# One scratch buffer for the first rotation, and the third token block's row sums ahead of the last pair's tokens

## The chip, the core and the metric

The kernel runs on one core of a Trainium2 chip. The metric is the device time of one execution in microseconds (us). Before the change its median is 719.28 us over 3 runs (718.72 to 720.0).

A core has five engines, each with its own queue of instructions that it takes in order: TensorE (PE in the profile; matmuls and transposes), VectorE (DVE), ScalarE (ACT), GpSimd (POOL) and SyncE (SP, which here only issues transfers). TensorE's weight loads are listed apart as PEld. Transfers are carried out by DMA engines, which all queues share. An instruction can wait on counters ("semaphores") that other engines or landed transfers raise.

## The reference

Attention with rotary embedding over 4 batches, 8 heads, 576 positions and head size 64, and then a gated feed-forward layer over the 2304 tokens that attention gives (512 wide, 1536 hidden), all in float32:

```
q_rot, k_rot = (rotate(q), rotate(k))          # x1*cos - x2*sin, x1*sin + x2*cos
scores = q_rot @ k_rot^T / sqrt(64);  scores -= max;  attn = exp(scores)
attn = attn / (sum(attn) + 1e-9);     x = attn @ v  -> [2304, 512]
g = x @ w_gate;   silu = g / (1 + exp(-g));   val = x @ w_val
out = (silu * val) @ w_out
```

## The kernel before

Values are split into a high and a low part (`hi`, `lo`), and each product is made of two or three matmuls on the parts. The 32 heads are worked on as 16 pairs of heads. A pair has 9 blocks of 128 query rows; each block is scored against all 576 keys, its row maximum is taken (VectorE, L358), the exponential is taken with row sums (ScalarE, L376), E is transposed (TensorE, L419), split again (L420, L421), and multiplied with the values (L459). The unnormalised results go to a DRAM area `yd`, the reciprocals of the row sums to a DRAM area `rd`. The feed-forward part then loads tokens from `yd`, multiplies them with row sums from `rd`, splits them and runs the gate and value products (12 "units" by plain products, L776; the rest with a scheme of seven block products, L824), and at last the output product (L892, L941).

The opening, `start` (L210), rotates the first pair. The rotation `turn` (L182) makes four tensor-tensor steps: two products with the sine table into a scratch (L200), one with the cosine table into `rot` (L201), one add (L202). Keys and the first quarter of the queries are rotated by VectorE (L229, L232), the other three quarters of the queries by GpSimd (L233). VectorE's scratch `tp` and a small scaled table `td` are taken from the pool of scores buffers (`sc_p`, two buffers of 128x1024 in PSUM), which are not yet in use. ScalarE fills `td` (L230) and the scaled query table `tab[0]` (L231), which GpSimd's rotation reads. TensorE then transposes keys, tails and the first query quarter, ScalarE and VectorE split them (L302, L306), and `scores(0)` runs; then the three other query quarters are transposed (L253), and `scores(1)`, `scores(2)` follow. The order on each engine in `start` is as written, up to small moves by the scheduler.

The second place is `plain` (L1196), the first part of the feed-forward layer. At its start (L1227 to L1234) SyncE issues loads in the order written: weights, tokens of blocks 1 and 2 of the second batch pair for the first three head pairs of each batch (`yload(1, 0)`, `yload(2, 0)`), row sums (`rload(1, 1)`, and `rload(1, 2)` into `R12`, a piece of buffer `T2l`), and the tokens of the last head pair of each batch (`yload(1, 1)`, `yload(2, 1)`). `rload` (L602) for the third token block issues six loads, `yload` (L632) four: two into `T0h` (`Ya`), two into `T2h` (`Yb`). `xlate(1)` and `xlate(2)` (L640) then combine them: for each of four groups c, ScalarE copies Ya (L649), VectorE adds Yb (L650) and multiplies with the row sums (L651), ScalarE and VectorE split (L656, L659). `ev(u)` (L780) empties a unit's PSUM on ScalarE (L791, L792) and issues its store from ScalarE's own queue (L799, L802).

Transfers are counted with eight counters, named DMAHW0 to DMAHW7 in the order below. They are given out in turn to transfers of SyncE and ScalarE alike, and the instruction that issues a transfer waits until the transfer before it on the same counter has landed. The suffixes on names, as in `yd_58`, are buffer numbers.

Of the kernel before, what the change touches and what calls it, by code (L numbers as in the profile page):

```python
# [10 lines left out]
FP32 = mybir.dt.float32  # L11
# [6 lines left out]
B, H, S, D = 4, 8, 576, 64  # L18
# [77 lines left out]
def r32(ap):  # L96
    return ap.bitcast(FP32)
# [10 lines left out]
class Attn:  # L108
# [101 lines left out]
    def start(self):  # L210
        nc = self.nc
        ve, po = nc.vector, nc.gpsimd
        rot = self.rot[0] = self.rot_p.tile([128, NSLOT, D], FP32, name="rot")
        rf = rot.rearrange("p s d -> p (s d)")
        T = nc.tensor.transpose
        tr = lambda: self.tr_p.tile([128, 512], FP32, name="tr")
        hi = lambda *x: self.qk_hi(0, *x)
        lo = lambda *x: self.qk_lo(0, *x)
        pw = self.pv_p.tile([128, 512], FP32, name="pv")

        def warm(n):
            for _ in range(n):
                nc.tensor.matmul(pw[:, 0:128], self.ident, self.ident, start=True, stop=True)
        w = PLAN["warm"]
        nc.scalar.copy(self.et_p.tile([128, 640], FP32, name="Et")[:, 0:1], r32(self.BD[0])[:, 0, 0:1])
        warm(w[0])
        self.turn(po, 0, 2)
        tp, td = (self.sc_p.tile([128, 1024], FP32, name="sc").rearrange("p (s d) -> p s d", d=D) for _ in range(2))
        self.turn(ve, 0, 1, 0, 4, tp[:, 0:8])  # L229
        nc.scalar.mul(td[:, 0:2], self.tab[1][:, :, 0], float(D ** -0.5))  # L230
        nc.scalar.mul(self.tab[0], self.tab[1], float(D ** -0.5))  # L231
        self.turn(ve, 0, 0, 0, 1, tp[:, 8:10], td[:, 0:2, None])  # L232
        self.turn(po, 0, 0, 1, 4)  # L233
        pk, pt, pq = tr(), tr(), tr()
        kt = lambda i: T(pk[:, i * 128:(i + 1) * 128], rf[:, 512 + i * 128:640 + i * 128], self.ident)
        for o in (64, 0):
            T(pt[:, o:o + 128], rf[:, 1024:1152], self.ident)
        warm(w[1])
        for i in range(4):
            kt(i)  # L240
        warm(w[2])
        T(pq[:, 0:128], rf[:, 0:128], self.ident)
        for x in ((pt, None, 192), (pk, 640, 512), (pq, 64, 128)):
            hi(*x)
        for x in ((pt, None, 192), (pk, 640, 512), (pq, 64, 128)):
            lo(*x)
        nc.scalar.copy(self.VS[0][:, :, 0:64], self.VR)
        warm(w[3])
        self.scores(0, False, lambda x: warm(w[4]) if x == 0 else None)
        self.peak(0)  # L250
        ps = tr()
        for i in range(1, 4):
            T(ps[:, i * 128:(i + 1) * 128], rf[:, i * 128:(i + 1) * 128], self.ident)  # L253
        self.scores(1, False)
        hi(ps[:, 128:512], 192, 384)
        lo(ps[:, 128:512], 192, 384)
        self.peak(1)
        self.exp(0)
        self.exp(1)
        warm(w[5])  # L260
        self.scores(2)
        self.exp(2)
        del self.rot[0], self.X[0]
        self.load_qk(2)
        self.qk_stack(0)
# [708 lines left out]
def attn_swiglu(ctx: ExitStack, tc: tile.TileContext, qk, vr, wg, wv, wo, main, tail, out):  # L974
# [163 lines left out]
    moe.open_chain(cctx, 2, side="right")  # L1138
    moe.open_aux(xctx, 2)
    J, S, Z = plain(moe, ps, cv1[1])  # L1140
    mctx.close()
    pl.close()
# [12 lines left out]
def run(ops, n=99):  # L1155
    while ops and n:
        ops.pop(0)()
        n -= 1
# [37 lines left out]
def plain(moe, ps, first):  # L1196
    nc = moe.nc
    ve, po = nc.vector, nc.gpsimd
    J = [Conv(moe, 1 + s // 2, s % 2, s % 2) for s in range(10)]
    jobs = []  # L1200

    def job(kind, x, h=0):
        if kind == "w":
            jobs.append((lambda: J[x].load(h), lambda: J[x].bits(h, ve)))
        else:
            jobs.append((lambda: moe.oload(x), lambda: moe.obits(x)))

    for s in range(10):
        for h in range(2):
            job("w", s, h)  # L1210
        if s in (4, 6, 8):
            job("o", 2 + s // 2)
    for f in (0, 1, 2, 3, 7, 8, 9, 10, 11):
        job("o", f)
    S = Stream(moe, jobs)
    ps = {1: ps}

    def mm(u):
        ps[u] = [moe.mm(*UNITS[u], i) for i in range(2)]

    def ev(u):
        moe.ev(u, ps.pop(u))

    def T1(c):
        run(moe.split(ve, *(t[:, :, c] for t in moe.T[1]), moe.Z[c]))

    S.load()  # L1227
    S.load()
    moe.yload(1, 0)
    moe.rload(1, 1)  # L1230
    moe.yload(2, 0)
    moe.yload(1, 1)
    moe.rload(1, 2, moe.R12)
    moe.yload(2, 1)  # L1234
    run(first())
    for c in range(2):
        run(moe.forms(1, c, moe.Z[c], po))
    x1, x2 = moe.xlate(1), moe.xlate(2)
    mm(2)
    S.sign()  # L1240
    run(S.take(1))
    ev(1)
    mm(3)
    run(S.take(1, False))
    run(J[0].sums(po))
    ev(2)
    mm(4)
    ev(3)
    mm(5)
    run(x1, 5)  # L1250
    ev(4)
    mm(6)
    run(x1)
    ev(5)
    mm(7)
    T1(0)
    run(x2, 3)
    ev(6)
    mm(8)
    w = [J[0].split(x, po) for x in range(2)]  # L1260
    run(w[0])
    run(x2, 2)
    ev(7)
    mm(9)
    run(w[1])
    run(x2)
    ev(8)
    mm(10)
    T1(1)
    Z = [moe.r_p.tile([128, 4, BK], FP32, name="R"), moe.again("T0l0", [128, 4, BK], FP32, "Z")]  # L1270
    for c in range(2):
        run(moe.forms(0, c, Z[c], po))
    T2 = moe.forms2(ve)
    run(T2, 2)
    ev(9)
    mm(11)
    run(T2)
    ev(10)
    S.sign()
    run(S.take(1))  # L1280
    ev(11)
    return J, S, Z
# [106 lines left out]
```

## Time and profile before

| what | value |
|---|---|
| median of 3 runs | 719.28 us |
| profiled execution, its own time | 719.76 us |
| its span, first to last instruction | 717.9 us |
| PE busy | 697.0 us (97%), 4342 matmuls |
| DVE / ACT / POOL busy | 540.6 / 409.6 / 476.8 us |
| mean granted TensorE clock | 0.994 of full speed |
| DMA | 143.86 MB, mean 200 GB/s |

The span leaves out 1.86 us that the device time holds (719.76-717.9). A timeline row gives the start and the duration in us, the engine, the line of the kernel, the operation, what it writes and reads, and in brackets how long the engine had been idle before it and what ended that. "SPq" and "ACTq" are the queues that issue transfers. A busy TensorE is not TensorE at its peak, and matmuls overlap, so the duration of a group includes its drain.

### The profile page before, as it was taken

The numbers are of one execution on the slowest core, as the hardware profiler recorded it, in microseconds if no ns is written. First come the engines' busy times: TensorE is split into PE (matmuls) and PEld (weight loads), VectorE is DVE, ScalarE is ACT, GpSimd is POOL, SyncE is SP. The second block draws the span as 40 slices with busy tenths as digits, with TensorE's granted clock in tenths as the row PEclk, the third lists the DMA queues.
The fourth block names the chain that finished last, engine by engine and source line by source line (L and its number), as shares of the span: only waits on it lengthen the run. The fifth ranks groups of instructions, "written<-read, shape, count | busy, mean of one in ns | idle before, by whom it ended". The sixth has DMA issues, their size and how long they took to land.

```text
span 717.9 us, 12738 instructions
## 1 busy us (share of the span) xinstructions
PE 697.0 (97%) x4342; PEld 656.7 (91%) x4342; DVE 540.6 (75%) x884; ACT 409.6 (57%) x892; POOL 476.8 (66%) x473
## 2 busy tenths in 40 slices
PE   7999999999999999998899999999999999999997
PEld 6999999999999998988899999999999877888887
DVE  5889898898898887848988778778677893464451
ACT  5889988888888886357433534424243332432331
POOL 8899799999999966649966576655675767200000
PEclk9999999999999999999999999999999999999999
DMA  6798899779887896862355555645638865787671
GB/s 195 195 232 204 218 227 253 199 202 249 233 215 196 201 269 165 248 202 101 121 168 171 177 163 173 193 147 165 185 115 272 280 245 169 306 284 223 205 220 30
DMA packets 111330, 143.86 MB, mean 200 GB/s; under 512 B 17809, under 2 KB 86049, under 8 KB 111265
## 3 DMA queue, kind: packets, MB, share of 16 engines
q1 hardware_dynamic: 106576, 137.64, 67.5%
q10 hardware_dynamic: 4688, 5.39, 2.3%
q8 instruction: 35, 0.57, 0.3%
q14 instruction: 31, 0.25, 0.1%
HBM read 76.35 MB, written 42.54 MB: 166 GB/s over the span
## 4 chain that ended last, share of the span: by engine, by line
PE 64%; DMA 10%; POOL 10%; DVE 8%; ACT 5%; issue 2%; SPq 1%; ACTq 0%; DVEq 0%; POOLq 0%
PE ch L824 28%; PE ch L941 13%; PE sc L343 7%; PE pv L459 6%; PE tr L419 5%; DMA HF<-hf 3%; PE ch L892 2%; POOL t L200 1%; DMA raw<-in_moe_w_gate_dram 1%; DMA QK<-N 1%; POOL rot L202 1%; DMA ht<-sv 1%; POOL rot L201 1%; PE tr L283 1%; POOL Xab L628 1%
## 5 line engine op out<-in xcount | busy, mean ns | idle before, releaser
L358 DVE TENSOR_REDUCE nmt<-sc 128x1 f32<-128x576 f32 x144 | 108.1, 751 | 20.0 <-PE sc L343 18.4
L376 ACT ACTIVATE E<-sc,nmt 128x576 f32<-128x576 f32 x128 | 97.3, 760 | 1.6 <-DVE nmt L358 1.4
L808 POOL TENSOR_TENSOR u<-u,z 128x384 f32<-128x384 f32 x30 | 30.5, 1018 | 72.9 <-DVE sg L808 72.9
L419 PE MATMUL tr<-ident,E 128*128 128x128 f32 x512 | 77.1, 273 | 0.5 <-DVE ET1l L421 0.2
L419 PEld LDWEIGHTS tr<-ident,E 128*128 128x128 f32 x512 | 61.1, 141 | 3.4 <-PE tr L283 1.3
L827 ACT COPY c<-ch 128x384 f32<-128x384 f32 x30 | 14.4, 480 | 84.7 <-PE ch L824 50.2
L200 POOL TENSOR_TENSOR t<-X,tab 128x256 f32<-128x256 f32 (+2 forms) x94 | 54.2, 597 | 10.1 <-DMA X<-in_qk_dram 6.4
L343 PE MATMUL sc<-QK 128*128 128x288 f32 x240 | 58.6, 325 | 1.7 <-ACT E L376 0.4
L420 ACT CAST ET2h<-tr 128x512 fp32r<-128x512 f32 x80 | 47.1, 589 | 15.5 <-PE tr L419 15.4
L421 DVE TENSOR_TENSOR ET2l<-tr,ET2h 128x512 fp32r<-128x512 f32 x80 | 53.1, 682 | 2.2 <-ACT ET2h L420 2.0
L678 DVE TENSOR_TENSOR hl<-hg,hh 128x384 fp32r<-128x384 f32 x44 | 25.8, 587 | 37.6 <-ACT hh L678 37.6
L941 PE MATMUL ch<-Oh,hh 128*128 128x512 f32 (+1 forms) x144 | 54.0, 375 | 0.0
L941 PE MATMUL ch<-Oh,hl 128*128 128x512 f32 (+1 forms) x144 | 53.9, 374 | 0.0
L941 PE MATMUL ch<-Ol,hh 128*128 128x512 f32 (+1 forms) x144 | 53.8, 374 | 0.0
L343 PE MATMUL sc<-N,QZ 128*128 128x288 f32 x240 | 51.3, 295 | 0.0
L202 POOL TENSOR_TENSOR rot<-rot,t 128x512 f32<-128x512 f32 (+2 forms) x47 | 47.0, 1000 | 3.7
L421 DVE TENSOR_TENSOR ET1l<-tr,ET1h 128x512 fp32r<-128x512 f32 x64 | 43.0, 685 | 6.8 <-ACT ET1h L420 6.5
L201 POOL TENSOR_TENSOR rot<-X,tab 128x512 f32<-128x512 f32 (+2 forms) x47 | 47.0, 1001 | 0.0
L808 DVE TENSOR_TENSOR sg<-ch,u 128x384 f32<-128x384 f32 x60 | 33.4, 556 | 16.5 <-PE ch L824 13.3
L678 ACT CAST hh<-hg 128x384 fp32r<-128x384 f32 x44 | 22.6, 514 | 39.3 <-DVE hg L928 39.3
L420 ACT CAST ET1h<-tr 128x512 fp32r<-128x512 f32 x64 | 36.9, 597 | 13.0 <-PE tr L419 13.0
L459 PE MATMUL pv<-ET2h,VS 128*128 128x320 f32 x128 | 40.7, 328 | 1.0 <-ACT ET2h L420 0.9
(413 smaller groups left out, 2418.9 us busy)
## 6 DMA issues: line engine op xcount, KB each, us to landing
QK<-N SPq DMA_DIRECT2D x64, 288.0 KB, 4.4
hg<-ht SPq DMA_DIRECT2D x22, 768.0 KB, 6.8
HF<-hf SPq DMA_DIRECT2D x12, 896.0 KB, 5.1
X<-in_qk_dram SPq DMA_DIRECT2D x15, 576.0 KB, 4.9
yd<-Y SPq DMA_DIRECT2D x31, 256.0 KB, 4.4
ht<-sg SPq DMA_DIRECT2D x20, 384.0 KB, 3.7
hf<-sg SPq DMA_DIRECT2D x20, 384.0 KB, 3.8
ht<-sg SPq DMA_DIRECT2D x20, 320.0 KB, 3.1
```

The costliest lines, as they stand in the source:

```text
L200: e.tensor_tensor(out=sel(t2, u), in0=sel(x, w), in1=tb(Sn, u), op=ALU.mult)
L201: e.tensor_tensor(out=o, in0=x, in1=tb(C, slice(0, D)), op=ALU.mult)
L343: nc.tensor.matmul(ps[:, g, 0:288], l, rr[:, o + g * 288:o + (g + 1) * 288], start=(x == 0), stop=(x == len(terms) - 1))
L358: nc.vector.tensor_reduce(out=nmcol, in_=ps[:, :, 0:288], axis=AX.XY, op=ALU.max, negate=True)
L376: nc.scalar.activation(out=E.rearrange("p (a b) -> p a b", a=2), in_=ps[:, :, 0:288], func=ACTF.Exp, bias=nmcol, scale=1.0, accum_out=self ...
L419: nc.tensor.transpose(ps[:, c], E[:, o + c * 128:o + (c + 1) * 128], self.ident)
L420: nc.scalar.copy(dst[0], src)
L421: nc.vector.tensor_tensor(out=dst[1], in0=src, in1=r32(dst[0]), op=ALU.subtract)
L459: nc.tensor.matmul(st["ps"][:, 0:w], VS[:, sl, :], t, start=(x == 0), stop=(x == last))
L808: add = lambda e, out, in0, in1: e.tensor_tensor(out=out, in0=in0, in1=in1, op=ALU.add)
L824: nc.tensor.matmul(acc, l[:, w, c * 128:(c + 1) * 128], r, start=(n == 0), stop=(n == 5))
L941: self.nc.tensor.matmul(ps, l[:, f], r[:, z], start=(n == 0), stop=(n == 3 * NFF - 1))
```

## The change

Two edits. In `start`, `td` is no longer a buffer of its own but columns 640 to 767 of the buffer that holds `tp`. In `plain`, the six loads of `rload(1, 2)` are issued ahead of the four of `yload(1, 1)`.

```
-        tp, td = (self.sc_p.tile([128, 1024], FP32, name="sc").rearrange("p (s d) -> p s d", d=D) for _ in range(2))
+        tp = self.sc_p.tile([128, 1024], FP32, name="sc").rearrange("p (s d) -> p s d", d=D)
+        td = tp[:, 10:12]
         self.turn(ve, 0, 1, 0, 4, tp[:, 0:8])
         nc.scalar.mul(td[:, 0:2], self.tab[1][:, :, 0], float(D ** -0.5))
         nc.scalar.mul(self.tab[0], self.tab[1], float(D ** -0.5))
         self.turn(ve, 0, 0, 0, 1, tp[:, 8:10], td[:, 0:2, None])
@@
     moe.yload(2, 0)
+    moe.rload(1, 2, moe.R12)
     moe.yload(1, 1)
-    moe.rload(1, 2, moe.R12)
     moe.yload(2, 1)
```

Line numbers after the first edit are one higher than before. On ScalarE, in the opening, the rows were these (a row: line, operation, output and inputs, shape, what it waits for); `sc<-tab_98` fills `td`, `tab_97` is the scaled query table:

```order
L225 COPY Et<-BD_95 128x1 [waits DVE_49]
L230 ACTIVATE sc<-tab_98 128x128 [waits DMAHW2_49]
L231 ACTIVATE tab_97<-tab_98 128x512
L302 CAST N_93<-tr 128x3x64 [waits PE_49]
L302 CAST N_93<-tr 128x512 [waits PE_49]
```

On ScalarE at the same place they are now:

```order
L225 COPY Et<-BD_95 128x1 [waits DVE_49]
L231 ACTIVATE sc<-tab_98 128x128 [waits DMAHW2_49,DVE_49]
L232 ACTIVATE tab_97<-tab_98 128x512
L303 CAST N_93<-tr 128x3x64 [waits PE_49]
L303 CAST N_93<-tr 128x512 [waits PE_49]
```

Nothing moved; the step that fills `td` has a wait for VectorE (`DVE_49`) that it did not have. On VectorE, in the opening, the rotation's rows were these:

```order
L201 TENSOR_TENSOR rot<-X,tab_98 128x2x4x64
L202 TENSOR_TENSOR rot<-rot,sc 128x2x4x64 [waits DVE_49]
L200 TENSOR_TENSOR sc<-X,sc 128x2x32 [waits DMAHW4_49,DVE_49,Activation_49]
L200 TENSOR_TENSOR sc<-X,sc 128x2x32 [waits DVE_49]
L201 TENSOR_TENSOR rot<-X,sc 128x128
L202 TENSOR_TENSOR rot<-rot,sc 128x128 [waits DVE_49]
```

On VectorE at the same place they are now:

```order
L201 TENSOR_TENSOR rot<-X,tab_98 128x2x4x64
L202 TENSOR_TENSOR rot<-rot,sc 128x2x4x64 [waits DVE_49]
L200 TENSOR_TENSOR sc<-X,sc 128x2x32 [waits DMAHW4_49,Activation_49]
L200 TENSOR_TENSOR sc<-X,sc 128x2x32 [waits DVE_49]
L201 TENSOR_TENSOR rot<-X,sc 128x128 [waits DVE_49]
L202 TENSOR_TENSOR rot<-rot,sc 128x128 [waits DVE_49]
```

The first `sc<-X,sc` waits for ScalarE alone of the two engines, and the step that reads `td` next has a wait for VectorE's own earlier step. On TensorE the third scores, `scores(2)`, and the first transposes of E that follow stood in this order; they are now interleaved, with two of the four transposes ahead of the last two score matmuls (two lines of the order, four transposes before as `x4`, now twice `x2`). On ScalarE the exponential of the sixth block now stands ahead of a cast of pair 1's rotated rows (L302) that stood before it. On GpSimd no row moved.

On SyncE, in `plain`, the rows from the last load of `yload(2, 0)` on were these (the ten that change places are the second to the eleventh; `T2l<-rd` is `rload(1, 2)`, `T0h` and `T2h` from `yd_58` first `yload(1, 1)`, then `yload(2, 1)`):

```order
L638 DMA T2h<-yd_57 64x3x384 [waits DMAHW4_49]
L638 DMA T0h<-yd_58 64x384 [waits DMAHW5_49]
L638 DMA T2h<-yd_58 64x384 [waits DMAHW6_49]
L638 DMA T0h<-yd_58 64x384 [waits DMAHW7_49]
L638 DMA T2h<-yd_58 64x384 [waits DMAHW0_49]
L613 DMA T2l<-rd 64x4x256 [waits DMAHW1_49,DVE_49,PE_49]
L613 DMA T2l<-rd 64x4x256 [waits DMAHW2_49]
L613 DMA T2l<-rd 64x4x64 [waits DMAHW3_49]
L613 DMA T2l<-rd 64x4x64 [waits DMAHW4_49]
L613 DMA T2l<-rd 64x4x64 [waits DMAHW5_49]
L613 DMA T2l<-rd 64x4x64 [waits DMAHW6_49]
L638 DMA T0h<-yd_58 64x384 [waits DMAHW0_49]
```

On SyncE at the same place they are now:

```order
L639 DMA T2h<-yd_57 64x3x384 [waits DMAHW4_49]
L614 DMA T2l<-rd 64x4x256 [waits DMAHW5_49,DVE_49,PE_49]
L614 DMA T2l<-rd 64x4x256 [waits DMAHW6_49]
L614 DMA T2l<-rd 64x4x64 [waits DMAHW7_49]
L614 DMA T2l<-rd 64x4x64 [waits DMAHW0_49]
L614 DMA T2l<-rd 64x4x64 [waits DMAHW1_49]
L614 DMA T2l<-rd 64x4x64 [waits DMAHW2_49]
L639 DMA T0h<-yd_58 64x384 [waits DMAHW3_49]
L639 DMA T2h<-yd_58 64x384 [waits DMAHW4_49]
L639 DMA T0h<-yd_58 64x384 [waits DMAHW5_49]
L639 DMA T2h<-yd_58 64x384 [waits DMAHW6_49]
L639 DMA T0h<-yd_58 64x384 [waits DMAHW0_49]
```

The six row-sum loads moved ahead of four token loads. The counters stay with the places: place two uses number 6 and place ten uses it again, whichever transfer stands there.

On ScalarE the store of `ev(5)`, `hf<-Xab` (L799), takes counter 6 next after the tenth load of these lists, before and now. Some rows ahead of it, ScalarE's copy of the last token group (L649, c=3) waits for counter 5 before, and now for counters 5 and 3: the loads at places nine and seven. VectorE's add behind it (L650) waits for the two `T2h` loads of the same `yload(1, 1)`, now at places eight and ten.

## Rows read from the trace of the kernel before

**Rows 1.** Busy time by stretch: span, then busy us of each engine, clock, DMA.

```profile
20.00:260.00 240.00, 236.38 (x1856) 228.72 (x1854) 211.63 (x342) 212.99 (x539) 221.17 (x255) 1.00 0.86 218
```

**Rows 2.** Timeline of the opening, all engines: start, duration, engine, line.

```profile
5.31 0.28 ACT L230 ACTIVATE sc<-tab 128x128 f32<-128x128 f32 x1 [2.17 <-DMA tab<-in_rope_dram]
...
5.53 0.61 ACT L231 ACTIVATE tab<-tab 128x512 f32<-128x512 f32 x1
...
6.28 1.53 POOL L200 TENSOR_TENSOR t<-X,tab 128x192 f32<-128x192 f32 x2 [1.32 <-ACT tab L231]
...
6.84 0.69 DVE L202 TENSOR_TENSOR rot<-rot,sc 128x512 f32<-128x512 f32 x1
...
7.58 0.65 PE L235 MATMUL tr<-ident,rot 128*128 128x128 f32 x4 [0.45 <-DVE rot L202]
7.62 0.49 DVE L200 TENSOR_TENSOR sc<-X,sc 128x64 f32<-128x64 f32 x2
...
8.84 1.00 POOL L202 TENSOR_TENSOR rot<-rot,t 128x384 f32<-128x384 f32 x1
...
9.38 1.05 PE L343 MATMUL sc<-N 64*128 64x288 f32 x6
...
10.37 0.55 PE L253 MATMUL tr<-ident,rot 128*128 128x128 f32 x3
...
13.23 0.42 PEld L419 LDWEIGHTS tr<-ident,E 128*128 128x128 f32 x4 [0.17 <-issue]
```

**Rows 3.** Timeline of SyncE's queue: the ten loads that change places.

```profile
299.09 0.47 SPq L638 DMA_DIRECT2D T0h<-yd  x1
303.96 0.47 SPq L638 DMA_DIRECT2D T2h<-yd  x1
...
305.53 0.44 SPq L638 DMA_DIRECT2D T2h<-yd  x1
306.08 4.33 SPq L613 DMA_DIRECT2D T2l<-rd  x6
```

**Rows 4.** Timeline of VectorE (first row) and ScalarE around the store.

```profile
308.02 0.57 DVE L650 TENSOR_TENSOR aux<-aux,T2h 128x384 f32<-128x384 f32 x1 [0.89 <-ACT aux L649]
...
307.50 0.48 ACT L649 COPY aux<-T0h 128x384 f32<-128x384 f32 x1 [0.48 <-DVE xa2l L659]
...
310.34 0.50 ACT L792 COPY Xab<-ch 128x384 f32<-128x384 f32 x1
314.94 0.34 ACTq L799 DMA_DIRECT2D hf<-Xab  x1
315.33 1.47 ACT L678 CAST T1h<-T0l 128x1536 fp32r<-128x1536 f32 x1 [4.49 <-DMA T2l<-rd]
...
320.45 0.51 ACT L791 ACTIVATE Xab<-ch 128x384 f32<-128x384 f32 x1
```

**Rows 5.** Single transfers issued at 306.1, 303.96, 311.94, 299.09: size, us to landing.

```profile
T2l<-rd SPq DMA_DIRECT2D x1, 256.0 KB, 5.0
...
T2h<-yd SPq DMA_DIRECT2D x1, 96.0 KB, 2.6
...
T2h<-yd SPq DMA_DIRECT2D x1, 96.0 KB, 3.5
...
T0h<-yd SPq DMA_DIRECT2D x1, 96.0 KB, 6.2
```

**Rows 6.** TensorE's waits from 300 to 375 us: total, times, longest.

```profile
PE ch L824 <- DVE T0l L678: 1.8, 1, 1.8
PE ch L776 <- ACT Xab L791: 1.5, 1, 1.5
```

**Rows 7.** Busy time by stretch, columns as in rows 1.

```profile
318.00:322.00 4.00, 2.46 (x15) 2.14 (x14) 3.59 (x7) 1.63 (x4) 0.00 (x0) 1.00 0.47 179
354.00:358.00 4.00, 2.17 (x13) 1.86 (x12) 3.64 (x4) 2.00 (x3) 3.92 (x4) 1.00 0.63 184
358.00:362.00 4.00, 4.00 (x16) 4.00 (x15) 3.11 (x6) 2.87 (x6) 4.00 (x4) 0.57 0.00 0
```

More of the change, by code (lines that the diff above doesn't have):

```diff
@@ L227, in start @@
         self.turn(po, 0, 2)
-        tp, td = (self.sc_p.tile([128, 1024], FP32, name="sc").rearrange("p (s d) -> p s d", d=D) for _ in range(2))
+        tp = self.sc_p.tile([128, 1024], FP32, name="sc").rearrange("p (s d) -> p s d", d=D)
+        td = tp[:, 10:12]
         self.turn(ve, 0, 1, 0, 4, tp[:, 0:8])
@@ L1231, in plain @@
     moe.yload(2, 0)
+    moe.rload(1, 2, moe.R12)
     moe.yload(1, 1)
-    moe.rload(1, 2, moe.R12)
     moe.yload(2, 1)
```

## The prediction

> **What bounds the kernel now.** I first read the table of busy time by stretch [rows 1]. TensorE works 236.38 of the 240 us between 20 and 260 us at granted clock 1.00: in the attention phase a delay that reaches TensorE has 3.62 us of idle time, and no more, in which it could vanish. Then I read the opening of the timeline [rows 2], where the scratch edit lies. The program starts there as one chain: the rope table lands, VectorE and GpSimd rotate the first pair, TensorE transposes, ScalarE splits, TensorE multiplies. Third comes the SyncE queue around 300 us [rows 3], where the moved loads are issued, and ScalarE and VectorE over the same stretch [rows 4]. The reader should see there that ScalarE, ready at 310.34+0.50=310.84, issues its next store only at 314.94, and that the row behind that store carries 4.49 us of waiting on a `T2l<-rd` load. That is the shared counter shown in the order: the store's counter, number 6, was last used by the sixth row-sum load. Last, TensorE's waits [rows 6]: 1.5 us for a buffer that the ScalarE row at 320.45 empties, and 1.8 us for the T0l split. Around 300 to 360 us the ScalarE and VectorE chain, not TensorE, sets the pace.
>
> **Part one, the scratch in one buffer.** It removes one buffer from the rotation and adds two waits. The buffer saves nothing: the first scores (the row at 9.38 in [rows 2]) wait for ScalarE's last split, not for a buffer, and the two buffers simply swap roles afterwards.
>
> The first new wait stands on ScalarE's multiply into `td`. It started at 5.31, and the order now has it wait for VectorE. Which VectorE step is not printed. But the wait for VectorE that stood on the following `sc<-X,sc` is gone, so the new one must cover the same step: the last that reads the first scratch, the add at 6.84, which ends at 7.53. The transposes that wait for that same add start at 7.58, so I put the lag at 0.05 us and the multiply at 7.58. Behind it in ScalarE's queue stands the scaling of the query table: 5.53 becomes 7.80 and it ends 0.61 us later, at 8.41. Who waits for that is GpSimd, whose three quarters of the query rotation start 0.14 us after it (5.53+0.61=6.14 to 6.28): 6.28 becomes 8.55, or +2.27. Its last add ends at 8.84+1.00+2.27=12.11.
>
> Who waits for that is TensorE: the three transposes at 10.37 become 12.16, +1.79 us. In before GpSimd was ready at 9.84, so 0.53 us of the 2.27 is swallowed there. In TensorE's order all later scores stand behind these transposes. What comes ahead, the first scores at 9.38, slips by less: `sc<-X,sc` goes from 7.62 to about 7.91 and the second new wait, between VectorE's own steps, adds about 0.1, so some 0.4. The scores end near 10.83, and TensorE then stands idle for 12.16-10.83=1.33 us, a gap that before did not have.
>
> The reordered transposes of E cost at most two more changes between 64-row and 128-row weights. The row at 13.23 shows 0.17 us of issue idle at such a change, so 0 to 0.34 us. I take 0.2: the neighbours overlap partly. The later cast of pair 1 on ScalarE I cost at nothing; what hides it is that its stacked copy is read a pair later. If that cover went, one cast of about 0.6 us would show. Part one is 1.79+0.2=+2.0 us, with bounds 1.8 to 2.1 if it lasts. It should last, since everything behind is fed by the same delayed start and TensorE's idle time up to 260 us is 3.62 us in all [rows 1].
>
> **Part two, the row sums ahead of the tokens.** No byte is added; ten transfers change places on one queue. Before, the ten began at 299.09 (first token load), then 303.96, and the six row-sum loads ran from 306.08, 4.33/6=0.72 us each [rows 3]. The order keeps the counters by place, so the second place still opens at 303.96 and the fourth at 305.53. After: row sums at 299.09, 303.96, 304.68, 305.53, 306.25 and 306.97, token loads from 307.7, half a microsecond each (the 0.47 of [rows 3]). The last token load, place ten, must also see the 256 KB row-sum load of place two landed: 303.96+5.0 [rows 5] = 308.96, so it is issued near 309.2.
>
> The nearest rows for how long its 96 KB take are 2.6, 3.5 and 6.2 us [rows 5]. I take 3.5, the one issued while a ScalarE store was under way, because that store, held by the third row-sum load's counter until 304.68+5.0=309.7, will be too. The load lands at 312.7, bounds 311.8 to 315.4.
>
> Who waits for it: the token step c=3. Before, its VectorE add ran at 308.02 and ScalarE was ready to store at 310.84, 2.82 us later [rows 4]. After, the add starts at 312.75 and ScalarE is ready at 315.57 against 314.94: +0.63 us. The wait on the counter is gone, and a wait for the data has taken its place. Bounds: -0.3 (landing at 311.8) to +3.3 (at 315.4). Queued behind are T1h, the second rotation of tokens and the emptying at 320.45 that TensorE waits for [rows 4, 6], so a shift there reaches the end one for one. That the row sums themselves land earlier serves nobody: their first reader on VectorE stands behind T1h, which starts at 315.33 [rows 4].
>
> [...]
>
> **Sum.** 2.0+0.6=+2.6 us. On the profiled execution, 719.76 (span 717.9 and 1.86 outside it), that is 722.36; that execution is 0.48 above the median of 719.28, so I forecast 721.9. The likeliest case's own range is 720.8 to 724.
>
> **Rivals.**
> 1. *The new gap costs the clock.* TensorE at 1.33 us idle could fall to its lower level. [...] Price: 4 us x 0.43=1.7 us, so 723.6. [...]
> 2. *The start's delay is swallowed*, by TensorE's 3.62 us of idle time before 260 us and the waits after it. For it: some of that idle time is waiting for transfers. Against: those transfers are issued behind the same delayed work. Then only part two is left: about 719.9, no change.
> 3. *The tokens land late*, at 315.4, beside the store: +3.3 instead of +0.6, so 724.6.
> 4. *Faster*: the counter's wait disappears and nothing replaces it. ScalarE would store at 310.84, 4.1 us earlier, so 719.28+2.0-4.1=717.2. It decides where the last token load lands before 310.84-2.87=307.97; against it, the load is issued only near 309.2. That the order of the queue yields no benefit at all is inside my forecast.
>
> **Chances.** Forecast 0.55, clock 0.15, swallowed 0.14, late tokens 0.09, faster 0.07. About 0.2% (1.44 us) is what a measurement of this kernel can tell from no change: faster means under 717.84, slower over 720.72. That gives slower 0.79, same 0.14, faster 0.07. The range runs from 719.8, which takes in most of the swallowed case, to 724.8, just past the late one.
>
> **What would show it.** In the changed profile: ScalarE's two scalings near 7.6 and 7.8 instead of 5.31 and 5.53; a GpSimd idle of about 3.6 us ahead of the query rotation; the three transposes near 12.2; a TensorE gap of about 1.3 us before them, and the clock there. Each later landmark, the last attention product for instance, then sits 2 us later; if it does not, rival 2 holds. Around 300 us, with that 2 us taken off, ScalarE's copy of the last token row should start near 312 instead of 307.50 and its store come right behind without waiting on a row-sum load. The forecast is wrong if the three transposes are not late, or if that store comes much before 314.

## The result, and the profile after

The changed kernel takes 728.11 us (median of 16 runs), the kernel before, timed beside it, 719.21 (16 runs). The medians are 8.9 us apart. The ratio is 1.0107, 95% interval 1.0079 to 1.0134, or +7.7 us with 5.7 to 9.6; it lies nearer to the ratio of the means, and so under that of the medians. The forecast was 721.9 with 724.8 as its upper end: slower was right, the size was not.

A median hides here that the runs of the changed kernel form two groups, and the rest can't be read without it: four take 721.07 to 722.74 (mean 721.83, clock .996 to .998), twelve take 725.12 to 731.31 (mean 728.47, mean granted clock .984 to .988 and once .994). The 16 runs of before lie within 716.70 and 721.95. The profiled execution is one of the twelve (730.06, span 728.2).

The opening of the timeline of after, all engines (start, duration, engine, line, in brackets the idle time before), answers to [rows 2]:

```profile
7.59 0.28 ACT L231 ACTIVATE sc<-tab 128x128 f32<-128x128 f32 x1 [4.44 <-DVE rot L202]
7.80 0.61 ACT L232 ACTIVATE tab<-tab 128x512 f32<-128x512 f32 x1
...
8.55 1.14 POOL L200 TENSOR_TENSOR t<-X,tab 128x192 f32<-128x192 f32 x2 [3.59 <-ACT tab L232]
...
9.09 0.33 PE L243 MATMUL tr<-ident,rot 128*128 128x128 f32 x1 [0.60 <-DVE rot L202]
...
9.79 1.06 PE L344 MATMUL sc<-N 64*128 64x288 f32 x6
...
10.73 0.99 POOL L202 TENSOR_TENSOR rot<-rot,t 128x384 f32<-128x384 f32 x1
...
11.77 0.55 PE L254 MATMUL tr<-ident,rot 128*128 128x128 f32 x3 [0.93 <-POOL rot L202]
```

ScalarE's two scalings, GpSimd's start and the late transposes stand where the prediction put them, but for one size: GpSimd's two products took 1.14 us in place of 1.53, so the transposes are at 11.77 and not 12.16, and TensorE's new wait is 0.93 us, not 1.33. The wait between VectorE's own steps, put at about 0.1, cost 0.12: L201 starts 0.03 us behind the end of L200 (8.42, and 7.90+0.49=8.39), in before 0.09 ahead of it (8.02, and 7.62+0.49=8.11). What TensorE's wait brought stands in the busy time by stretch (length, TensorE's busy us with its instructions, granted clock, DMA). The first row is of before, the others are of after:

```profile
14.00:30.00 16.00, 15.70 (x118) 1.00 0.83 186
...
10.00:12.00 2.00, 1.07 (x8) 1.00 0.19 23
...
13.00:14.00 1.00, 1.00 (x6) 0.62 0.68 277
14.00:30.00 16.00, 16.00 (x62) 0.50 0.52 115
30.00:31.00 1.00, 1.00 (x10) 0.85 0.06 16
31.00:60.00 29.00, 28.51 (x220) 1.00 0.87 222
```

A clock of 0.62 from 13 to 14 us and of 0.85 from 30 to 31 puts the fall at 13.2 and the return at 30.3, if the clock is 0.50 between them and 1.00 outside. For these 17.1 us TensorE runs at its lower level, a granted clock of 0.50, busy all the time, and from 14 to 30 us it does 62 instructions where before did 118. Over the three rows from 13 to 31 us, 0.38+8+0.15=8.5 us of full clock are missing.

SyncE's queue, ScalarE, VectorE and the matmul that waits, in the timeline of after around the moved loads, answer to [rows 3, 4]:

```profile
308.07 8.10 SPq L614 DMA_DIRECT2D T2l<-rd  x6
316.21 0.61 SPq L639 DMA_DIRECT2D T0h<-yd  x1
...
321.54 0.48 ACT L650 COPY aux<-T0h 128x384 f32<-128x384 f32 x1 [5.65 <-DMA T0h<-yd]
...
322.05 0.57 DVE L651 TENSOR_TENSOR aux<-aux,T2h 128x384 f32<-128x384 f32 x1 [6.07 <-ACT aux L650]
...
324.38 0.50 ACT L793 COPY Xab<-ch 128x384 f32<-128x384 f32 x1
324.91 0.34 ACTq L800 DMA_DIRECT2D hf<-Xab  x1
...
330.97 0.44 PE L777 MATMUL ch<-xa2h,w0h 128*128 128x384 f32 x1 [1.98 <-ACT Xab L792]
```

The store comes right behind the emptying; the 4.49 us on a `T2l<-rd` load of [rows 4] are gone, and ScalarE waits 5.65 us for the tokens instead. TensorE's waits from 278 to 345 us, answering to [rows 6]:

```profile
PE ch L777 <- ACT Xab L792: 2.6, 2, 2.0
```

Landmarks of the two profiled executions show where the 10.3 us of span came in:

| landmark (line of before) | before | after | later by |
|---|---|---|---|
| first matmul of L776 | 277.9 | 286.5 | 8.6 |
| store of `ev(5)`, L799 | 314.94 | 324.91 | 10.0 |
| first matmul of L824 | 339.5 | 349.5 | 10.0 |
| first of L892 | 561.4 | 569.9 | 8.5 |
| first of L941 | 622.1 | 632.4 | 10.3 |

So 8.6 us come in ahead of the feed-forward part, of which the late opening can account for 2, and 1.4 at the moved loads. The clock can account for the 1.5 given back before L892: the fall at 358 to 362 of [rows 7], 4x0.43=1.7 us of full clock, has no match in this execution, whose clock is 1.00 from 346 us to the last matmul. The 1.8 lost again behind it stand beside 1.9 us more of waiting for GpSimd (L679); this was not followed up.

### The profile page after: what moved, and what is told of

Read it like the earlier page. It is cut to its first block, busy times and chain, and to the rows that moved or that the text cites. A ratio compares the mean times of both kernels' runs of the same rounds, so it can differ in the third digit from the quotient of the medians.

```text
span 728.2 us, 12738 instructions
## 1 busy us (share of the span) xinstructions
PE 703.8 (97%) x4342; PEld 661.4 (91%) x4342; DVE 539.7 (74%) x884; ACT 409.2 (56%) x892; POOL 476.1 (65%) x473
## 4 chain that ended last, share of the span: by engine, by line
PE 74%; DVE 8%; DMA 7%; ACT 6%; POOL 2%; issue 2%; SPq 1%; ACTq 0%; DVEq 0%; POOLq 0%
PE ch L825 26%; PE ch L942 13%; PE pv L460 11%; PE sc L344 11%; PE tr L420 8%; DMA HF<-hf 3%; PE ch L893 2%; PE tr L284 2%; ACT E L377 1%; DMA ht<-sv 1%; POOL fl L679 1%; DVE HF L883 1%; ACT N L303 1%; PE ch L777 1%; DVE T2l L679 1%
## 5 line engine op out<-in xcount | busy, mean ns | idle before, releaser
L420 PE MATMUL tr<-ident,E 128*128 128x128 f32 x512 | 79.6, 279 | 0.4 <-DVE ET1l L422 0.2
L420 PEld LDWEIGHTS tr<-ident,E 128*128 128x128 f32 x512 | 62.6, 144 | 4.0 <-issue 1.5
L200 POOL TENSOR_TENSOR t<-X,tab 128x256 f32<-128x256 f32 (+2 forms) x94 | 53.5, 591 | 18.7 <-DMA X<-in_qk_dram 12.7
L679 DVE TENSOR_TENSOR hl<-hg,hh 128x384 fp32r<-128x384 f32 x44 | 25.8, 587 | 38.7 <-ACT hh L679 38.7
L202 POOL TENSOR_TENSOR rot<-rot,t 128x512 f32<-128x512 f32 (+2 forms) x47 | 46.9, 999 | 3.7
L201 POOL TENSOR_TENSOR rot<-X,tab 128x512 f32<-128x512 f32 (+2 forms) x47 | 47.2, 1005 | 0.0
L679 ACT CAST hh<-hg 128x384 fp32r<-128x384 f32 x44 | 22.6, 514 | 40.0 <-DVE hg L929 40.0
```

Of the source, the lines that this page charges most:

```text
L200: e.tensor_tensor(out=sel(t2, u), in0=sel(x, w), in1=tb(Sn, u), op=ALU.mult)
L420: nc.tensor.transpose(ps[:, c], E[:, o + c * 128:o + (c + 1) * 128], self.ident)
L679: return [lambda: self.nc.scalar.copy(h, f), lambda: le.tensor_tensor(out=l, in0=f, in1=r32(h), op=ALU.subtract)]
```

## The experiments

All were timed beside the kernel before: scratch_only, swap_only, tab_first and gap_filled on one chip, late_gpsimd, rows_last and both_filled on a second, later_gpsimd and half_filled on a third. "Above 724" is taken as the count of executions in which the clock fell as in the profile above: their mean clock is .981 to .991, but for one of after (725.12, .994), and none at or under 724 is below .992. Of 96 runs of the kernel before none is above 724 (highest 721.95).

| kernel | median us (runs) | ratio to before, 95% | above 724 |
|---|---|---|---|
| after | 728.11 (16) | 1.0107, 1.0079 to 1.0134 | 12 |
| scratch_only | 725.78 (12) | 1.0065, 1.0035 to 1.0094 | 7 |
| swap_only | 721.00 (11) | 1.0024, 1.0009 to 1.0039 | 0 |
| tab_first | 720.35 (12) | 1.0013, 0.9992 to 1.0033 | 1 |
| gap_filled | 719.61 (12) | 1.0001, 0.9989 to 1.0013 | 0 |
| half_filled | 719.91 (12) | 1.0018, 0.9996 to 1.0041 | 1 |
| late_gpsimd | 720.22 (12) | 1.0034, 1.0009 to 1.0059 | 3 |
| later_gpsimd | 729.43 (5) | 1.0147, 1.0126 to 1.0168 | 5 |
| both_filled | 721.63 (11) | 1.0046, 1.0032 to 1.0060 | 0 |
| rows_last | 718.76 (12) | 1.0007, 0.9992 to 1.0023 | 0 |

**scratch_only** is the kernel before with the first hunk of the change alone (`td = tp[:, 10:12]`).

> The second area of the first rotation lies in the scores buffer of the first, the order of SyncE's loads is that of the kernel before. Theory (TensorE's wait for GpSimd's rotation near 11 us drops its clock): in most executions TensorE runs at the lower clock (0.50) from about 13 to 30 us and the time is 725 to 729; in a few the clock holds and the time is 720.5 to 721.2; the median lies 6 to 8 us above the kernel before. Rival 1 (the clock belongs to the moved loads, or to both parts together): 720.5 to 721.2 in every run, +1.4 to +2.0, clock 1.00 from 13 to 30 us. Rival 2 (the delay of the opening is swallowed and the excess lies at the loads): within 0.5 of the kernel before.

Seven executions at 725.17 to 727.74, five at 718.89 to 720.71: the two groups come with the scratch edit. The profiled execution happens to be one of the five. TensorE's late transposes in its timeline, and the transpose before them, without a wait here:

```profile
8.79 0.33 PE L243 MATMUL tr<-ident,rot 128*128 128x128 f32 x1
...
11.47 0.55 PE L254 MATMUL tr<-ident,rot 128*128 128x128 f32 x3 [0.80 <-POOL rot L202]
```

And TensorE's busy time by stretch, columns as above:

```profile
10.00:12.00 2.00, 1.20 (x9) 1.00 0.28 39
12.00:14.00 2.00, 2.00 (x13) 1.00 0.68 265
14.00:30.00 16.00, 15.69 (x113) 1.00 0.80 179
```

The wait is there and the clock held. The wait doesn't bring the fall each time. The five others were expected at +1.4 to +2.0; their mean of 719.65 is 0.6 over the mean of before (719.10), a miss that is taken up below.

**swap_only** is the second hunk alone (`rload(1, 2)` ahead of `yload(1, 1)`).

> Only SyncE's order is changed: the third block's six row-sum loads stand ahead of the four loads of the last pair's tokens. Theory: the first rotation is as before, the clock is 1.00 from 13 to 30 us, and the store of the fifth step begins 0.6 to 1.1 us later than before: 719.8 to 720.3, +0.6 to +1.1. Rival (the loads carry the excess of the whole change, their lateness growing to the end): +4 or more, 723 to 728.

The ratio gives +1.7 us (0.6 to 2.8), and no execution is above 722.51. The median is 0.7 over the 720.3 that was expected at most. SyncE, VectorE, ScalarE and TensorE in its timeline (line numbers as in before):

```profile
299.20 8.11 SPq L613 DMA_DIRECT2D T2l<-rd  x6
...
313.22 0.57 DVE L650 TENSOR_TENSOR aux<-aux,T2h 128x384 f32<-128x384 f32 x1 [6.12 <-DMA T2h<-yd]
...
316.07 0.34 ACTq L799 DMA_DIRECT2D hf<-Xab  x1
...
322.14 0.44 PE L776 MATMUL ch<-xa2h,w0h 128*128 128x384 f32 x1 [1.98 <-ACT Xab L791]
```

**gap_filled** leaves the late GpSimd as it is and fills TensorE's wait.

```
(scratch_only, in start)
         self.peak(0)
+        warm(6)
         ps = tr()
```

> As scratch_only, with six identity products of 128x128 put on TensorE between the first scores and the three query transposes that wait for GpSimd; they cost nothing beyond the wait, since they lie in it. Theory (TensorE's idle stretch is what drops the clock): the transposes come as late as in scratch_only (11.8 to 12.2 us), but the clock stays 1.00 from 13 to 30 us in all executions and the time is +1.4 to +2.0, 720.6 to 721.2, some 6 us under scratch_only. Rival (what drops the clock is the lateness of the opening against something else, not the idle stretch): as scratch_only, with the fall near 13 us still there, +6 to +8.

TensorE's opening in its timeline, where the fill (L223; each product has two entries) took 1.60 us, more than the wait; the last row is its busy time from 14 to 30 us, columns as in [rows 1]:

```profile
9.17 0.33 PE L243 MATMUL tr<-ident,rot 128*128 128x128 f32 x1 [0.60 <-DVE rot L202]
...
9.88 1.06 PE L345 MATMUL sc<-N 64*128 64x288 f32 x6
10.87 1.60 PE L223 MATMUL pv<-ident 128*128 128x128 f32 x12
12.31 0.49 PE L255 MATMUL tr<-ident,rot 128*128 128x128 f32 x3
...
322.03 0.44 PE L778 MATMUL ch<-xa2h,w0h 128*128 128x384 f32 x1 [0.20 <-ACT Xab L793]
...
14.00:30.00 16.00, 15.68 (x112) 13.35 (x112) 12.61 (x20) 12.32 (x32) 15.29 (x21) 1.00 0.79 177
```

The transposes are later than in after (12.31 against 11.77), and yet none of 12 executions is above 721.17, against 7 of 12 of scratch_only on the same chip. In these runs the fall goes with TensorE's idling, not with the lateness; the wait of 0.60 us ahead of the transpose at 9.17, which after has too, did not do it in this execution.

**half_filled** has `warm(3)` in place of `warm(6)`.

> As gap_filled with three identity products in place of six: they cover about 0.45 of TensorE's wait and leave 0.35 to 0.5. If the length of the wait decides how likely the fall is: 0 to 2 of 12 executions above 724, the median 719.5 to 720.5. If any wait at this place will do: as scratch_only, about 7 of 12 above 724 and the median there too.

The expectation misjudged the fill: three products took 0.94 us and left 0.06 of the wait, so this repeats gap_filled rather than tries a shorter wait. One of 12 executions was above 724 (728.42, clock .981); it was not the profiled one, and what TensorE did in it is not seen.

**tab_first** exchanges ScalarE's two scalings, so that GpSimd isn't held.

```
(scratch_only, in start)
+        nc.scalar.mul(self.tab[0], self.tab[1], float(D ** -0.5))
         nc.scalar.mul(td[:, 0:2], self.tab[1][:, :, 0], float(D ** -0.5))
-        nc.scalar.mul(self.tab[0], self.tab[1], float(D ** -0.5))
```

> As scratch_only, but ScalarE scales the table of the queries (tab[0]) ahead of the column that waits for VectorE, so GpSimd's rotation is not held. Theory (GpSimd's lateness makes the gap, and the gap the fall of the clock): GpSimd begins its query products near 6.3 us as before, the key transposes come 0.4 us late (VectorE's second rotation still waits), the three query transposes stand right behind the first scores, the clock is 1.00 from 13 to 30 us, and the time is +0.2 to +0.6, 719.4 to 719.8. Rival (VectorE's waits in the shared buffer cause the loss, not GpSimd's): as scratch_only, +1.4 to +8.

In the profiled execution the transposes stand right behind the scores (10.33, before 10.37) and the clock holds (1.00 from 10 to 60 us). Eleven executions lie at 717.65 to 721.60, one at 726.92. The theory holds for the eleven; the one is open, as in half_filled.

**late_gpsimd** makes the wait without the scratch edit.

```
(before, in start)
+        z = self.t_p.tile([128, 8, D], FP32, name="t2")
+        for _ in range(5):
+            po.memset(z, 0.0)
         self.turn(po, 0, 0, 1, 4)
```

> The kernel before (two scores buffers, SyncE's order as before) with one thing added: five fills of a 128x512 scratch tile on GpSimd ahead of its query rotation, which then begins some 1.0 to 1.4 us later; nothing that VectorE or ScalarE do waits for more than before. Theory (the idle stretch of TensorE ahead of the three query transposes drops the clock, whatever makes it): executions fall apart as in scratch_only, a part of them at a clock of .984 to .988 and some 7 us longer, 725 to 728, the others 719 to 720.5. Rival (the fall belongs to the shared scores buffer, that is to VectorE's and ScalarE's waits or to the other order of the instructions behind it): no execution over 722, clock .994 or more in all of them.

GpSimd and TensorE in its timeline:

```profile
5.01 2.87 POOL L235 MEMSET t<- 128x512 f32 x5
7.96 1.15 POOL L200 TENSOR_TENSOR t<-X,tab 128x192 f32<-128x192 f32 x2
...
8.67 0.33 PE L245 MATMUL tr<-ident,rot 128*128 128x128 f32 x1 [0.22 <-DVE rot L202]
...
11.20 0.55 PE L256 MATMUL tr<-ident,rot 128*128 128x128 f32 x3 [0.77 <-POOL rot L202]
```

And TensorE's busy time by stretch:

```profile
10.00:12.00 2.00, 1.23 (x9) 1.00 0.37 71
12.00:14.00 2.00, 2.00 (x13) 0.93 0.71 258
14.00:16.00 2.00, 2.00 (x7) 0.50 1.01 192
...
24.00:26.00 2.00, 2.00 (x10) 0.50 0.31 124
26.00:28.00 2.00, 2.00 (x13) 0.66 0.03 8
```

Here nothing is shared, and three of 12 executions fall (724.75 to 726.18; the profiled one is among them). The rival, that the fall belongs to the shared buffer, is out. Set beside scratch_only: nearly the same wait (0.77 and 0.80 us), nearly the same busy time from 10 to 12 us (1.23 and 1.20), and the clock fell in the one and held in the other. The two openings are not alike ahead of that, though: here TensorE also waits 0.22 us ahead of the transpose at 8.67, and in scratch_only's profiled execution it does not wait there at all. One profile of each can't tell whether such small waits decide or chance.

**later_gpsimd** has ten fills.

> As late_gpsimd with ten fills in place of five (0.57 each there, so 2.9 more): TensorE's wait ahead of the three query transposes grows from 0.77 to about 3.6. Open is why only part of the executions fall (3 of 12 there, 7 of 12 in scratch_only). If the length of the wait decides how likely the fall is: in all or nearly all of 12 executions the clock falls near 13 us, and the time is 726 to 731. If it is a matter of chance that the length doesn't move: again 3 to 7 of 12 above 724, the rest near 721 to 722.5 (the delay alone, +2.5 to +3.7, of which up to half is lost again before the fifth step's store).

All five executions fall (728.46 to 730.93, clock .985 to .988); 12 were expected, five were timed. TensorE's wait in its timeline:

```profile
14.08 0.55 PE L256 MATMUL tr<-ident,rot 128*128 128x128 f32 x3 [2.92 <-POOL rot L202]
```

And TensorE's busy time by stretch, where the lower level begins and ends:

```profile
14.00:16.00 2.00, 1.92 (x9) 0.66 0.72 265
...
28.00:30.00 2.00, 2.00 (x10) 0.50 0.00 0
30.00:32.00 2.00, 2.00 (x12) 0.58 0.00 0
```

So the fall was likelier with the longer wait (5 of 5 against 3 of 12, on another chip). By 0.66 and 0.58 the lower level runs from 14.6 to 31.7 us, 17.0 us as in after; in late_gpsimd, by 0.93 and 0.66, from 13.7 to 27.4, or 13.6 us.

**both_filled** is the whole change with `warm(6)` at the same place.

> The whole change, with six identity products of 128x128 put into TensorE's wait ahead of the three query transposes. Theory (the median's excess over the forecast is the fall of the clock, and that comes from the idle stretch alone): no execution at a clock under .990; the time is that of gap_filled and swap_only together, 721.0 to 722.0, +2.0 to +3.0 over the kernel before and 6 to 7 us under the change as it is. Rival (the moved loads make the fall likelier or have an excess of their own on top of the late opening): 724 or more.

721.00 to 723.91, no fall, +3.3 us (2.3 to 4.3). The median is 3.0 over that of the kernel before, where that of after was 8.9 over it, so the fill takes off about 6 us. What is left is what the four executions of after with the clock held show (mean 721.83 there, 721.89 here). The matmul behind the store, in its timeline:

```profile
323.82 0.51 PE L778 MATMUL ch<-xa2h,w0h 128*128 128x384 f32 x1 [1.99 <-ACT Xab L793]
```

**rows_last** tries the order of loads that the reasons point to: `rload(1, 2)` behind `yload(2, 1)`.

> The kernel before with the third block's six row-sum loads moved the other way, behind all eight loads of the last pair's tokens. Theory (the fifth step's store on ScalarE is held by the landing of the load that shares its counter, and by the tokens' landing): the last of those tokens lands 1 to 2 us earlier, the store begins near 313.5 instead of 314.94 us, and the time is 1.0 to 1.4 us less, 717.6 to 718.2. Rival 1 (another wait stands right behind: the row sums are now the late ones, or the gain is swallowed behind 326 us): within 0.4 of the kernel before. Rival 2: the row sums come so late that the third block waits, +0.5 to +3.

ScalarE's store and the step behind it, in its timeline:

```profile
313.93 0.34 ACTq L799 DMA_DIRECT2D hf<-Xab  x1
314.31 1.47 ACT L678 CAST T1h<-T0l 128x1536 fp32r<-128x1536 f32 x1 [3.83 <-DMA T2l<-rd]
```

The store is 1.0 earlier than in [rows 4], but it still ends a wait on a row-sum load, and the time is not seen to be shorter: +0.5 us, with -0.6 to +1.7, where -1.0 to -1.4 was expected. The gain, if there is one, is too small for 12 runs. No version tried beats the kernel before.

## Why the prediction was wrong

**The step that failed is rival 1**: its chance, .15, and its price, "4 us x 0.43=1.7 us, so 723.6". The mechanism was named and its place was right. It happened in 12 of 16 executions and cost 6.6 us (728.47-721.83); in scratch_only 7.2 (726.85-719.65). The price was taken from the fall at 358 to 362 [rows 7], where 0.43 of the clock was missing, as if each fall lasted as long. This one lasted 17 us. The chance was set by comparing two late stretches of four us [rows 7], the one at 354, with 2.17 us busy and a clock of 0.57 behind it, and the one at 318, with 2.46 us busy and 1.00; a third was passed over. The trace of before has a second fall (columns as in rows 1):

```profile
326.00:330.00 4.00, 1.71 (x7) 0.82 (x5) 2.86 (x6) 2.74 (x7) 3.23 (x2) 1.00 0.29 98
330.00:334.00 4.00, 3.83 (x13) 3.83 (x14) 3.48 (x5) 3.59 (x4) 4.00 (x3) 0.59 0.29 98
```

It speaks for the fall and against so low a chance, but not for the price: at a clock of 0.59 for 4 us, and 0.99 in the next 4, it is about as short as the one at 358. What the range left out is a fall of another length early in the attention phase. There TensorE is the bound, with 3.62 us of idle time in 240 [rows 1], and the fall is paid for the greater part. Of the 8.6 us at the first landmark, 2.1 are the late opening (280.0 in scratch_only, where the clock held, against 277.9), which leaves 6.5 for the 8.5 us of clock that are missing in after.

**Without the fall the sum holds.** The forecast's +2.6 (721.9) stands against 721.83 in the four executions and against +3.3 (2.3 to 4.3) in both_filled. Its terms are less well met than their sum, so that the sum comes out is in part luck.

- *Part one, +2.0.* Through the attention phase it holds: the first matmul of L776 is late by 2.1 in scratch_only and by 2.3 in gap_filled (280.2). "It should last" failed. With the order of loads as before, TensorE's wait ahead of the matmul at 321.01 (the 1.5 of [rows 6]) shrinks from 1.54 us in before, the row below, to 0.20 in gap_filled, and that matmul is late by 1.02 only (322.03). So rival 2 happened in half, at a wait that the prediction had listed, and the whole of gap_filled is at +0.1 (-0.8 to +0.9). By the trace half of the 2 us is swallowed there. Where the rest goes stays open: the short falls behind 320 us, two in before's profiled execution (0.59 at 330 to 334, 0.57 at 358 to 362), one in gap_filled's (0.60 at 330 to 334) and none in scratch_only's (mean clock 1.000), can shift the later landmarks by up to 1.7 us each (4x0.43).

```profile
321.01 0.44 PE L776 MATMUL ch<-xa2h,w0h 128*128 128x384 f32 x1 [1.54 <-ACT Xab L791]
```

- *Part two, +0.6.* The chain is as put: the add at 313.22 (forecast 312.75), the store at 316.07 (315.57), no wait on a row-sum load. That is +1.13 in place of +0.63, within the bounds of -0.3 to +3.3, and +1.7 (0.6 to 2.8) in device time. The late-token rival (3) did not happen: the add is 2.2 us ahead of its 315.4.
- *In the traces the parts don't simply add.* The matmul at 321.01 comes 1.02 later with the scratch edit filled, 1.13 with the swap, and 2.81 with both (323.82). With the swap TensorE's wait stays at 1.98 or 1.99 us, so the opening's delay finds no slack there. In device time this is not shown: +3.3 (2.3 to 4.3) for both, against 0.1+1.7=1.8, lies within what the three intervals allow.

Rival 4 is out: the wait on the counter went, and the wait for the tokens took its place.

Open are: why executions of one and the same program form two groups; why the lower level lasted 13.6 to 17.1 us in the opening and less than 4 us at 358, and at 330 about as short; and what happened in the two single executions above 724, of tab_first and half_filled, whose profiled sisters have no wait or 0.06 us of one ahead of the late transposes.

## What to carry to other kernels

Price a new wait of TensorE not by its own length alone but by what it can do to the clock, and don't take a fall to last as long as those that the trace happens to show: two lasted less than 4 us there, the new one 17. A wait of less than 1 us cost 6.6 to 7.2 us here, in some executions and not in others. Where such a wait can't be avoided, put idle products into it (1.6 us of identity products left no fall in 23 executions), and time enough executions to see both groups. When two edits delay the same chain, look for the slack between them: the first may be free only because the second isn't there.

## What was not expected of the hardware

- The clock's lower level lasted from 13.2 to 30.3 us in after, 13.7 to 27.4 in late_gpsimd and 14.6 to 31.7 in later_gpsimd, with TensorE busy 16.00 of 16 us from 14 to 30 in after. In before a fall at 358 us was over within 4 us (0.57 from 358 to 362 [rows 7], 1.00 from 362 to 366).
- Executions of one and the same kernel differ in whether the clock falls: it fell in 12 of 16 with a wait of 0.93 us, 7 of 12 with 0.80, 3 of 12 with 0.77, 5 of 5 with 2.92, each wait read from one profiled execution.
- GpSimd's first two products took 1.53 us in before, where they start at 6.28 us, and 1.13 to 1.15 in the kernels in which they start at 7.96 to 10.87. In before VectorE's add L202 of the keys (6.84 to 7.53) runs beside them [rows 2]; whether that is why was not tested.
